# Joins of tiles 0 to 2 moved behind the branch, in front of the additions of their selected rows

## The chip, the cores and the metric

The kernel runs on one core of a Trainium2 chip. Its time is the device time in microseconds of one execution; the figure for a kernel is the median of its timed runs. TensorE does the matrix products, VectorE, ScalarE and GpSimd the elementwise work, and SP, a queue of its own, issues most of the DMA transfers. GpSimd issues the indirect ones. Each engine works through its own instructions in their written order, and waits at an instruction until the counters that it names (semaphores) have been reached.

## What is computed

Three stages follow each other on 2304 tokens of 512 values: attention, a mixture of eight experts, and a gated feed-forward layer. The change lies where the second stage passes into the third.

```
out = x.copy()
xc = x[x @ w_skip > 0]
e_idx, gate_w = ...                      # best expert of each token and its weight
for e in range(8):
    mask = e_idx == e
    h = np.maximum(xc[mask] @ w1[e], 0.0)
    y[mask] = gate_w[mask, None] * (h @ w2[e])
out[x @ w_skip > 0] = xc + y             # second stage
g = out @ w_gate
return (silu(g) * (out @ w_val)) @ w_out # third stage
```

## The kernel before

The tokens lie in 18 tiles of 128. Each expert has room for 192 of them. Its results are written to a table `ys` in HBM, one row for each place, and come back to the tokens' order by a gather.

**The last expert.** Its 192 rows are a short part (64 rows, product `yb`) and a long part (128 rows, product `ya`, made in two halves of 256 columns). Each product is copied to SBUF by `y_put_short` (on VectorE) or `y_put_long` (on ScalarE), and from there SP writes it to `ys`; the first write of `yb` and those of `ya` stand in SP's order behind the earlier gathers, which read the same table. So that tiles 0 to 2 need not wait for these writes, their rows of the last expert are not gathered: `sel_y` makes two fp16 parts of each product (`sely`; the high part on ScalarE, the rest on VectorE), and `sel_p(i)` picks the rows by a product with a matrix of zeros and ones (`selx`) on TensorE.

**A tile is put together in two steps.** The *join* `xp_1(i)` adds the gathered rows of the first seven experts, times the gate's weight, to the tokens; the addition at the end of `sel_p(i)` adds the selected rows of the last expert to the same tile `xr[i]`:

```
def xp_1(i):
    t = xg[i]
    dve.scalar_tensor_tensor(out=t if i > 2 else xr[i], in0=t, scalar=gw[:, i:i + 1], in1=xr[i], ...)   # L1213
def sel_p(i):
    p = bank([128, DM], "selx")          # eight products of 256 columns, L1132 and L1134
    ...
    dve.scalar_tensor_tensor(out=xr[i], in0=p, scalar=gw[:, i:i + 1], in1=xr[i], ...)                   # L1135
def y_put_long(e, o, n):
    t = t2.tile([128, n], F32, tag="t2", name="ya")
    hi_(t, yp.pop((e, 0)), 2.0 ** -8)    # copy on ScalarE, L340
    sp.dma_start(out=ys[r:r + 128, o:o + n], in_=t)                                                     # L1096
```

**Behind the branch.** A branch (L1599) asks whether an expert has more than 192 tokens; it is not taken here. Behind it tile 0 is transposed on TensorE (`xp_p`, product `xpp`), copied to `xpT` in fp16 by ScalarE (`xp_h`), and the rest of the rounding is put beside it by VectorE (`xp_l`); then come `gvp`, the projections of the third stage (`gv_part`, 128 tokens at a time for the first block), and so on for tiles 1 and 2. GpSimd gathers the rows of tiles 3 and up (`xp_g`).

**Conversion steps.** The third stage's weights are doubles and are turned into two fp16 parts on the way. A step `conv_next` works on three pieces at once: ScalarE rounds the piece finished by VectorE and GpSimd takes its rest (`w`), VectorE puts together the second (L1166 and L1167, `stg` and `cb`), ScalarE scales the third (L1159, L1160).

**What sets the order.** This part is written out by hand: each engine gets its instructions in the order of the code. Buffers come from pools. The pool `t2` has 24, for gathered rows, `sely`, `ya`, `yb` and others; a new tile takes a buffer that is free by then in the code's order, and its first writer waits for all who used that buffer before, for DMAs by the counter of their queue. SP's DMAs use the counters DMAHW0 to DMAHW7 in turn, GpSimd's DMASW0 to DMASW7.

Of the kernel before, what the change touches and what calls it, by code (L numbers as in the profile page):

```python
# [307 lines left out]
def body(ctx, tc, qkt, vwin, vrow, w_skip, w_gate, w1, w2, g_w, v_w, o_w, cst, out, dbg=None):  # L308
# [78 lines left out]
    if True:  # L387
# [647 lines left out]
        def x_load(e):  # L1035
            t = m2.tile([128, 8, CAP], F16, tag="xe", name="xe")
            d = sp.dma_start_transpose(out=t, in_=xs[e * CAP:(e + 1) * CAP, :])
            rows_ready(d)
            xe[e] = t

        def h_step(e, m):
            if m == 0:
                hT[e] = pools["h6"].tile([128, 2, 8, CAP], F16, tag="h6", name="hT")
            p = bank([128, CAP], "hp")
            n = 0
            for kk in range(4):
                for wl, xl in ((0, 0), (0, 4), (1, 0)):
                    pe.matmul(out=p, lhsT=wt[e, kk][:, wl, m * 128:(m + 1) * 128], rhs=xe[e][:, xl + kk, :],  # L1048
                              start=(n == 0), stop=(n == 11))
                    n += 1  # L1050
            hi_(hT[e][:, 0, m, :], p, 1.0, AF.Relu)
            lo_(hT[e][:, 1, m, :], p, hT[e][:, 0, m, :], 0.0, ALU.max)

        def h_first():
            hT[0] = pools["h6"].tile([128, 2, 8, CAP], F16, tag="h6", name="hT")
            p = [bank([128, CAP], "hp") for m in range(8)]
            for kk in range(4):
                for m in range(8):
                    for n, (wl, xl) in enumerate(((0, 0), (0, 4), (1, 0))):
                        pe.matmul(out=p[m], lhsT=wt[0, kk][:, wl, m * 128:(m + 1) * 128], rhs=xe[0][:, xl + kk, :],  # L1060
                                  start=(kk == 0 and n == 0), stop=(kk == 3 and n == 2))
                w_step()
            for m in range(8):
                hi_(hT[0][:, 0, m, :], p[m], 1.0, AF.Relu)
                lo_(hT[0][:, 1, m, :], p[m], hT[0][:, 0, m, :], 0.0, ALU.max)
                if m in (1, 5):
                    w_step()
# [33 lines left out]
        def sel_make():  # L1101
            f = slp.tile([128, 3], F32, name="idf")
            dve.tensor_copy(f, idx[:, 0:3])
            d = t2.tile([128, 4, 128], F16, tag="t2", name="seld")
            pool.memset(d[:, 3, :], 1.0)
            for i in range(3):
                dve.tensor_scalar(out=d[:, i, :], in0=ident, scalar1=f[:, i:i + 1], scalar2=None, op0=ALU.mult)
            sel["d"] = d
# [18 lines left out]
        def sel_p(i):  # L1127
            p = bank([128, DM], "selx")
            for c in range(2):
                o = slice(256 * c, 256 * c + 256)  # L1130
                for n in range(2):
                    pe.matmul(out=p[:, o], lhsT=sel["o"][:, 0, i, :], rhs=sel[0][:, n, o], start=(n == 0), stop=False)  # L1132
                for n in range(2):
                    pe.matmul(out=p[:, o], lhsT=sel["o"][:, 1 + c, i, :], rhs=sel[1][:, n, :], start=False, stop=(n == 1))  # L1134
            dve.scalar_tensor_tensor(out=xr[i], in0=p, scalar=gw[:, i:i + 1], in1=xr[i], op0=ALU.mult, op1=ALU.add)  # L1135
            xg[i] = xr[i]
# [19 lines left out]
        def conv_a(kind, f, n):  # L1156
            t = sg64[kind, f, n].rearrange("p (c w) -> p c w", w=2)
            lo_w, hi_w = t[:, :, 0], t[:, :, 1]
            act.activation(out=hi_w.bitcast(F32), in_=hi_w.bitcast(F32), func=AF.Copy, scale=2.0 ** -111)  # L1159
            act.activation(out=lo_w, in_=lo_w.bitcast(U32), func=AF.Copy, scale=LOW_S, bias=LOW_B)  # L1160
            return cbp.tile([128, 512], I32, tag="cb", name="cb")

        def conv_b(kind, f, n, b):
            t = sg64.pop((kind, f, n)).rearrange("p (c w) -> p c w", w=2)
            lo_w, hi_w = t[:, :, 0], t[:, :, 1]
            dve.scalar_tensor_tensor(out=lo_w, in0=hi_w, scalar=-0x80000000, in1=lo_w, op0=ALU.bitwise_and, op1=ALU.bitwise_or)  # L1166
            dve.scalar_tensor_tensor(out=b, in0=hi_w, scalar=3, in1=lo_w, op0=ALU.logical_shift_left, op1=ALU.bitwise_or)  # L1167

        def conv_c(kind, f, n, b):
            if n == 0:  # L1170
                wm[kind, f] = (wq if nw[0] % 18 < NPRE else wps[0]).tile([128, 2, 2, 512], F16, tag="w", name="w")
                nw[0] += 1
            w, bf = wm[kind, f], b.bitcast(F32)
            hi_(w[:, 0, n, :], bf, 1.0)
            rest_(pool, w[:, 1, n, :], bf, w[:, 0, n, :])
# [7 lines left out]
        def loads64(q=sp):  # L1183
            while lq and nld[0] - ncv[0] + len(sg64) < 6 and len(lq) > keep[0]:
                load64(*lq.pop(0), q=q)

        def conv_next(ld=True):
            c = st_b.pop() if st_b else None
            b = st_a.pop() if st_a else None
            if c:  # L1190
                conv_c(*c)
            if b:
                conv_b(*b)
                st_b.append(b)
            if cq:
                a = cq.pop(0)
                st_a.append(a + (conv_a(*a),))
            if ld:
                loads64()
# [11 lines left out]
        def xp_1(i):  # L1211
            t = xg[i]
            dve.scalar_tensor_tensor(out=t if i > 2 else xr[i], in0=t, scalar=gw[:, i:i + 1], in1=xr[i], op0=ALU.mult, op1=ALU.add)  # L1213
            blk, o = divmod(i, 3)
            if o == 0 and i:
                xpT[blk] = pools["h6"].tile([128, 8, BLK], F16, tag="h6", name="xpT")

        def xp_p(i):
            p = bank([128, 4, 128], "xpp")
            for kk in range(4):  # L1220
                pe.transpose(out=p[:, kk, :], in_=xg[i][:, 128 * kk:128 * kk + 128], identity=ident)  # L1221
            xs_[i] = p
# [319 lines left out]
        def w_step():  # L1542
            if ncv[0] < 8 * E:
                w_conv(*divmod(ncv[0], 8))
                ncv[0] += 1
                loads()

        loads()
        for e in range(E):
            last = e == E - 1  # L1550
            if not last:
                x_load(e + 1)
            if e == E - 3:
                sel_make()
            if e == 0:
                h_first()
            for m in range(8 if e else 0):
                h_step(e, m)
                if m % 2:
                    w_step()  # L1560
                if last and m in (1, 4):
                    conv_next()
                if last and m == 1:
                    for i in range(3):
                        xp_g(i)
            if e == E - 3:
                sel_turn()
            y_short(e)
            if last:
                most = nc.values_load(flagi[0:1, 0:1], min_val=0, max_val=NT)  # L1570
                conv_next()
                sel_y(1, 0)
                y_put_short(e)
                for i in range(3):
                    xp_1(i)
                y_long(e, 0, DM // 2)
                sel_y(0, 0)
                y_put_long(e, 0, DM // 2)
                y_long(e, DM // 2, DM // 2)
                sel_y(0, DM // 2)  # L1580
                y_put_long(e, DM // 2, DM // 2)
            else:
                for n in range(3 if 0 < e < E - 3 else 2):
                    w_step()
                y_put_short(e)
                if e == E - 2:
                    conv_next(False)
                y_long(e, 0, DM)
                w_step()
                w_step()  # L1590
                y_put_long(e, 0, DM)
                if e == E - 2:
                    keep[0] = 0
                    conv_next()
# [11 lines left out]
        for i in range(3, 6):  # L1606
            xp_g(i)
        pp = [bank([128, BLK], "gvp") for n in range(2)]
        conv_next(False)
        sel_p(0)  # L1610
        sel_p(1)
        xp_p(0)
        xp_h(0)
        xp_l(0)
        sel_p(2)
        for i in range(3):
            if i < 2:
                xp_p(i + 1)
                xp_h(i + 1)
            gv_part(0, 0, pp, 128 * i, 128)  # L1620
            if i < 2:
                xp_l(i + 1)
# [49 lines left out]
        for n, (kind, b, f) in enumerate(seq):  # L1672
# [33 lines left out]
            if n in (4, 6, 8):  # L1706
                i = 4 + n // 2
# [53 lines left out]
```

## Time and profile before

| | us |
|---|---|
| Median of 3 runs | 748.16 (747.73 to 748.56) |
| Profiled execution | 746.42 |
| Its span, first to last instruction | 744.6 |
| TensorE busy | 704.0 |
| VectorE busy | 498.7 |
| ScalarE busy | 386.7 |

Positions in the trace are counted from the start of the span. The branch is passed at about 325 us. An engine's busy time is that of its instructions; waiting is not in it. The times of products on TensorE are modelled at their ends, so that an engine that looks busy may be held up a little more or less than shown.

### The profile page before, as it was taken

What the parts mean: (1) busy time and instruction counts of PE and PEld (TensorE: products, weight loads), DVE (VectorE), ACT (ScalarE), POOL (GpSimd) and SP (SyncE); (2) the same over time, 40 slices, a digit from 0 to 9 for tenths busy, and PEclk for the clock granted to TensorE, in tenths of its full rate; (3) what the DMA queues carried; (4) which work ended last, traced back from release to release, by engine and by line L of the source; (5) the groups of instructions that cost most, each with busy time, mean ns of one, the idle gap of its engine ahead of it and who ended that gap; (6) DMA issues with size and microseconds to landing.
All of it is one profiled execution on the core that took longest, in us unless ns stands there. A gap on an engine that the chain in (4) does not pass through costs nothing.

```text
span 744.6 us, 16389 instructions
## 1 busy us (share of the span) xinstructions
PE 704.0 (95%) x6567; PEld 466.7 (63%) x6567; DVE 498.7 (67%) x940; ACT 386.7 (52%) x766; POOL 282.6 (38%) x261
## 2 busy tenths in 40 slices
PE   8889788889899999989999899999999999999997
PEld 6677677778777888766665554455666666544443
DVE  6677587777688788769888989976668886300000
ACT  6565475452577776647777752445555655300000
POOL 5345575354100000236886775234434454200000
PEclk9999899999999999999999999999999999999999
DMA  8889887571799999865766511840000000001001
GB/s 258 246 267 273 190 208 197 149 176 50 230 353 341 346 364 284 269 218 183 217 179 187 155 27 42 163 92 1 2 0 1 1 1 1 1 28 43 29 29 42
DMA packets 95334, 108.82 MB, mean 146 GB/s; under 512 B 51248, under 2 KB 68658, under 8 KB 94679
## 3 DMA queue, kind: packets, MB, share of 16 engines
q1 hardware_dynamic: 91319, 99.80, 46.5%
q0 software_dynamic: 2880, 6.89, 2.9%
q10 hardware_dynamic: 1056, 1.05, 0.5%
q8 instruction: 52, 0.85, 0.5%
q14 instruction: 27, 0.22, 0.1%
HBM read 81.69 MB, written 17.30 MB: 133 GB/s over the span
## 4 chain that ended last, share of the span: by engine, by line
PE 42%; DVE 9%; ACT 3%; issue 3%; POOL 0%; ACTq 0%; DVEq 0%; POOLq 0%
PE p L1430 19%; PE op L1513 19%; PE gvp L1257 3%; DVE cb L1167 2%; DVE stg L1166 2%; DVE sg L1270 1%; DVE yg L1213 1%; DVE xphl L346 1%; ACT u L340 1%; ACT stg L1159 1%; ACT sg L1265 0%; DVE xpT L346 0%; ACT stg L1160 0%; PE xpp L1221 0%; ACT xpT L340 0%
## 5 line engine op out<-in xcount | busy, mean ns | idle before, releaser
L1513 PE MATMUL op<-w,u 128*128 128x512 f16 x648 | 140.2, 379 | 0.0
L1257 PE MATMUL gvp<-xpT,w 128*128 128x384 f16 (+1 forms) x720 | 111.1, 315 | 4.5 <-ACT sg L1265 2.2
L1513 PEld LDWEIGHTS <-u 128*128 128x128 f16 x648 | 63.5, 98 | 76.2
L1257 PEld LDWEIGHTS <-w 128*128 128x128 f16 x720 | 67.6, 98 | 47.2 <-issue 5.5
L343 DVE SCALAR_TENSOR_TENSOR w<-stg,w 128x1024 f16<-128x1024 f32 x64 | 79.7, 1273 | 17.9 <-ACT w L340 17.8
L346 POOL TENSOR_TENSOR w<-cb,w 128x512 f16<-128x512 f32 x36 | 52.2, 1450 | 83.6 <-ACT w L340 83.6
L1430 PEld LDWEIGHTS <-w 128*128 128x128 f16 x528 | 51.6, 98 | 36.1 <-issue 2.1
L340 ACT ACTIVATE w<-stg 128x1024 f16<-128x1024 f32 x64 | 65.7, 1051 | 16.0 <-DMA stg<-in_moe_w 14.6
L1048 PEld LDWEIGHTS <-w 128*128 128x128 f16 x672 | 55.7, 98 | 1.7
L1048 PE MATMUL hp<-xe,w 128*128 128x192 f16 x672 | 56.6, 246 | 0.0
L340 ACT ACTIVATE y<-op 128x512 f32<-128x512 f32 x18 | 10.7, 592 | 84.9 <-PE op L1513 84.4
L1430 PE MATMUL p<-t,w 128*128 128x384 f16 x244 | 50.1, 326 | 1.6 <-DVE sc L1303 1.6
L1430 PE MATMUL p<-xpT,w 128*128 128x384 f16 x264 | 46.5, 326 | 0.0
L1167 DVE SCALAR_TENSOR_TENSOR cb<-stg 128x512 int32<-128x512 int32 x36 | 42.1, 1171 | 3.5
L1430 PE MATMUL p<-t,s7h 128*128 128x384 f16 x176 | 42.9, 326 | 1.1 <-ACT sa L1454 1.1
L1083 PE MATMUL ya<-w,hT 128*128 128x512 f16 (+1 forms) x216 | 42.9, 356 | 0.0
L346 POOL TENSOR_TENSOR u<-sa,u 128x384 f16<-128x384 f32 x22 | 20.1, 915 | 49.9 <-ACT u L340 49.9
L1430 PEld LDWEIGHTS <-s7h 128*128 128x128 f16 x264 | 25.8, 98 | 18.3 <-issue 1.3
L511 PE MATMUL qkd<-qks,identh 128*128 128x192 f16 x192 | 34.7, 350 | 2.0 <-issue 2.0
L539 POOL TENSOR_TENSOR vr<-vr 72x1024 f32<-72x1024 f32 x8 | 18.8, 2356 | 41.7 <-DMA vr<-in_vr 38.4
L411 PE MATMUL wbank<-wz 128*128 128x252 bf16 x209 | 30.9, 287 | 2.5 <-POOL wz L407 1.3
L1083 PEld LDWEIGHTS <-hT 128*128 128x128 f16 x216 | 20.5, 98 | 20.3 <-issue 1.6
(196 smaller groups left out, 1389.8 us busy)
## 6 DMA issues: line engine op xcount, KB each, us to landing
stg<-in_moe_w SPq DMA_DIRECT2D x64, 512.0 KB
qk<-in_qk SPq DMA_DIRECT2D x24, 384.0 KB
stg<-in_moe_w_out SPq DMA_DIRECT2D x12, 512.0 KB
stg<-in_moe_w_gate SPq DMA_DIRECT2D x11, 512.0 KB
stg<-in_moe_w_val SPq DMA_DIRECT2D x11, 512.0 KB
vw<-in_vw SPq DMA_DIRECT2D x18, 284.4 KB
vr<-in_vr SPq DMA_DIRECT2D x8, 576.0 KB
up<-outd SPq DMA_DIRECT2D x18, 256.0 KB
```

Of the source, the lines that this page charges most:

```text
L340: act.activation(out=o, in_=i, func=func, scale=s)
L343: dve.scalar_tensor_tensor(out=o, in0=i, scalar=s, in1=h, op0=op, op1=ALU.subtract)
L346: eng.tensor_tensor(out=o, in0=i, in1=h, op=ALU.subtract)
L411: pe.matmul(out=wbank[:, 260:512], lhsT=wz[:, 0:128], rhs=wz[:, 0:252], start=True, stop=True)
L511: pe.matmul(out=p[:, n], lhsT=identh, rhs=qk_at(u, n, m // 4).rearrange("p b (g r) -> p b g r", r=4)[:, :, :, m % 4], start=(m == 0), stop ...
L539: pool.tensor_tensor(out=r[:, 0:2], in0=r[:, 0:2], in1=r[:, 2:4], op=ALU.add)
L1048: pe.matmul(out=p, lhsT=wt[e, kk][:, wl, m * 128:(m + 1) * 128], rhs=xe[e][:, xl + kk, :], start=(n == 0), stop=(n == 11))
L1083: pe.matmul(out=p, lhsT=hT[e][:, hl, m, 0:128], rhs=w[:, o:o + n], **f)
L1167: dve.scalar_tensor_tensor(out=b, in0=hi_w, scalar=3, in1=lo_w, op0=ALU.logical_shift_left, op1=ALU.bitwise_or)
L1257: pe.matmul(out=pp[n][:, o:o + width], lhsT=w[:, wl, n, kk * 128:(kk + 1) * 128], rhs=xpT[blk][:, xl + kk, o:o + width], start=(j == 0), s ...
L1430: pe.matmul(out=p, lhsT=l(wl)[:, 128 * kk:128 * kk + 128], rhs=rr(xl, kk), start=first and j == 0, stop=last and j == 5, skip_group_check= ...
L1513: pe.matmul(out=p, lhsT=u[:, ul, t * 128:(t + 1) * 128], rhs=w[:, wl, f % 2, :], start=(n == 0), stop=(n == 3 * NF - 1))
```

## The change

The three joins `xp_1(0)` to `xp_1(2)` leave their place ahead of the branch, between the short rows' copy and the products of the long rows. Behind the branch the first two stand directly in front of their `sel_p`, the third ahead of tile 0's transposes, which come before `sel_p(2)`. The conversion step that opened that group now ends it.

```diff
@@ -1571,8 +1571,6 @@
                 conv_next()
                 sel_y(1, 0)
                 y_put_short(e)
-                for i in range(3):
-                    xp_1(i)
                 y_long(e, 0, DM // 2)
                 sel_y(0, 0)
                 y_put_long(e, 0, DM // 2)
@@ -1606,13 +1604,16 @@
         for i in range(3, 6):
             xp_g(i)
         pp = [bank([128, BLK], "gvp") for n in range(2)]
-        conv_next(False)
+        xp_1(0)
         sel_p(0)
+        xp_1(1)
         sel_p(1)
+        xp_1(2)
         xp_p(0)
         xp_h(0)
         xp_l(0)
         sel_p(2)
+        conv_next(False)
```

No operation is added or left out. The lines behind the first hunk have numbers two lower in the changed kernel as far as the second hunk.

VectorE, directly behind the branch, by the built program; `x` is the tile that is put together, `yg` the gathered rows, a minus marks rows of before, a plus those of the changed kernel.

```order
-L1166 SCALAR_TENSOR_TENSOR stg<-stg 128x512
-L1167 SCALAR_TENSOR_TENSOR cb<-stg 128x512
-L1135 SCALAR_TENSOR_TENSOR x<-selx,gw,x 128x512 x2
+L1597 UNCONDITIONAL_BRANCH x2
+L1213 SCALAR_TENSOR_TENSOR x<-yg,gw,x 128x512
+L1135 SCALAR_TENSOR_TENSOR x<-selx,gw,x 128x512
+L1213 SCALAR_TENSOR_TENSOR x<-yg,gw,x 128x512
+L1135 SCALAR_TENSOR_TENSOR x<-selx,gw,x 128x512
+L1213 SCALAR_TENSOR_TENSOR x<-yg,gw,x 128x512
 L346 TENSOR_TENSOR xpT<-xpp,xpT 128x4x128
 L1135 SCALAR_TENSOR_TENSOR x<-selx,gw,x 128x512
+L1166 SCALAR_TENSOR_TENSOR stg<-stg 128x512
+L1167 SCALAR_TENSOR_TENSOR cb<-stg 128x512
 L346 TENSOR_TENSOR xpT<-xpp,xpT 128x4x128 x2
```

The first three joins now alternate with the additions, and the conversion's two rows (L1166, L1167) come after the third addition.

ScalarE, ahead of the branch, before: the high parts `sely` and the copies `ya` of the two halves of the long rows, with the counters that each waits for.

```order
L340 ACTIVATE sely<-yb 128x256 [waits DMAHW6_49,PE_49]
L340 ACTIVATE sely<-ya 128x256 [waits DMAHW6_49,PE_49,Activation_49]
L340 ACTIVATE ya<-ya 128x256 [waits DMASW2_49,DVE_49]
L340 ACTIVATE sely<-ya 128x256 [waits PE_49]
L340 ACTIVATE ya<-ya 128x256 [waits DMASW0_49,DMASW3_49,DVE_49,Pool_49]
```

ScalarE at the same place in the changed kernel:

```order
L340 ACTIVATE sely<-yb 128x256 [waits DMAHW6_49,PE_49]
L340 ACTIVATE sely<-ya 128x256 [waits DMAHW6_49,PE_49,Activation_49]
L340 ACTIVATE ya<-ya 128x256 [waits DMAHW5_49,DMAHW4_49,DMAHW7_49,DMAHW0_49,DVE_49]
L340 ACTIVATE sely<-ya 128x256 [waits PE_49]
L340 ACTIVATE ya<-ya 128x256 [waits DMAHW1_49,DVE_49]
```

The five instructions stand in the same order, but the two copies `ya` wait for other counters: the first for four of SP's DMA counters instead of one of GpSimd's, the second for DMAHW1.

SP at the same place in the changed kernel: a load of weights, the two writes of the short rows, and the two of the long rows. Each write also waits for the counter that it will itself raise, where that is not known to have been reached.

```order
L1145 DMA stg<-in_moe_w_val 128x4x256 [waits DMAHW0_49,DMAHW6_49,DVE_49,Activation_49]
L1090 DMA ys<-yb 64x256 [waits DMASW3_49,DMASW4_49,DMASW2_49,DVE_49]
L1090 DMA ys<-yb 64x256
L1096 DMA ys<-ya 128x256 [waits DMAHW1_49,Activation_49]
L1096 DMA ys<-ya 128x256 [waits DMAHW2_49,Activation_49]
```

These rows are the same before the change. The counters are taken in turn, so that the load raises DMAHW6, the writes of `yb` DMAHW7 and DMAHW0, and those of `ya` DMAHW1 and DMAHW2. The copy `yb` itself, on VectorE, waits for DMAHW5 and DMAHW4 in both kernels.

## Rows read from the trace of the kernel before

**Rows 1.** Page, part 1: each engine's busy time, share of the span, instructions.

```profile
PE 704.0 (95%) x6567; PEld 466.7 (63%) x6567; DVE 498.7 (67%) x940; ACT 386.7 (52%) x766; POOL 282.6 (38%) x261
```

**Rows 2.** Chain of waits behind the branch and later: start us, length us, what.

```profile
326.88 1.47 DVE x L1135 x2
...
328.37 0.04 ACTq L340
...
329.24 0.70 DVE xpT L346
...
423.67 15.76 PE gvp L1257 x96
```

**Rows 3.** Timeline, TensorE's later gaps: start, length, instruction, [idle before, releaser].

```profile
409.63 6.01 PE L1257 MATMUL gvp<-xpT,w 128*128 128x384 f16 x36 [0.95 <-ACT sg L1265]
416.38 6.01 PE L1257 MATMUL gvp<-xpT,w 128*128 128x384 f16 x36 [0.73 <-DVE sg L1270]
423.67 1.62 PE L1257 MATMUL gvp<-xpT,w 128*128 128x384 f16 x9 [1.29 <-ACT sg L1265]
```

**Rows 4.** Timeline, VectorE around the branch.

```profile
320.76 0.74 DVE L1213 SCALAR_TENSOR_TENSOR x<-yg,gw,x 128x512 f32<-128x512 f32 x1
...
322.85 0.75 DVE L1213 SCALAR_TENSOR_TENSOR x<-yg,gw,x 128x512 f32<-128x512 f32 x1 [0.23 <-DMA yg<-ys,idx]
323.52 0.42 DVE L343 SCALAR_TENSOR_TENSOR sely<-ya,sely 128x256 f16<-128x256 f32 x1
...
325.47 0.69 DVE L1166 SCALAR_TENSOR_TENSOR stg<-stg 128x512 int32<-128x512 int32 x1 [0.38 <-DVEq L1599]
...
333.93 0.69 DVE L346 TENSOR_TENSOR xpT<-xpp,xpT 128x512 f16<-128x512 f32 x1 [2.75 <-ACT xpT L340]
```

**Rows 5.** Timeline, ScalarE around the branch.

```profile
320.66 0.38 ACT L340 ACTIVATE sely<-ya 128x256 f16<-128x256 f32 x1 [2.02 <-issue]
323.97 0.39 ACT L340 ACTIVATE ya<-ya 128x256 f32<-128x256 f32 x1 [2.93 <-DVE sely L343]
...
325.17 0.38 ACT L340 ACTIVATE ya<-ya 128x256 f32<-128x256 f32 x1 [0.54 <-issue]
...
333.30 0.60 ACT L340 ACTIVATE xpT<-xpp 128x512 f16<-128x512 f32 x1 [3.02 <-PE xpp L1221]
```

**Rows 6.** SP's writes to `ys`, by tile (first and last start) and timeline.

```profile
L1090 SPq DMA_DIRECT2D ys<-yb x16: 461/582/935, 207.9 to 323.4; - x16
L1096 SPq DMA_DIRECT2D ys<-ya x9: 338/387/927, 210.7 to 325.6; - x9
...
324.38 1.54 SPq L1096 DMA_DIRECT2D ys<-ya  x2
```

**Rows 7.** Timeline, TensorE around the branch.

```profile
323.03 1.02 PE L1031 MATMUL warm<-cs 128*128 128x406 bf16 x5
325.65 0.38 PE L1132 MATMUL selx<-sely,sel 128*128 128x256 f16 x2 [1.60 <-ACTq L1599]
...
326.52 0.38 PE L1132 MATMUL selx<-sely,sel 128*128 128x256 f16 x2
```

**Rows 8.** Windows, all engines: last columns granted clock, DMA share, GB/s.

```profile
323.00:324.00 1.00, 1.00 (x7) 0.41 (x5) 0.94 (x2) 0.03 (x1) 0.00 (x0) 1.00 1.11 358
...
327.00:328.00 1.00, 0.87 (x9) 0.57 (x7) 1.00 (x2) 0.52 (x1) 0.00 (x0) 1.00 0.06 19
```

**Rows 9.** Timeline, GpSimd: the third gather's issue.

```profile
315.58 0.94 POOL L1205 DMA_INDIRECT yg<-ys,idx  x1 [0.30 <-issue]
```

**Rows 10.** DMA issues: times issued, median us from issue to landing.

```profile
xs<-xhl,idx POOLq DMA_INDIRECT x18, 2.6
```

**Rows 11.** Windows, TensorE alone: length, busy us, granted clock, DMA share, GB/s.

```profile
74.05:77.46 3.41, 1.76 (x38) 1.00 1.04 274
77.46:80.87 3.41, 3.41 (x49) 0.50 0.41 97
...
323.21:326.62 3.41, 1.81 (x14) 1.00 0.71 219
```

## The prediction

> **What bounds the kernel now.** I read the page first: TensorE is busy for 704.0 of the 744.6 us [rows 1]. Almost any stretch in which it waits is therefore lost to the end, and the question is what it waits for around the branch. The chain of waits answers that: just behind the branch it runs over two additions of selected rows on VectorE, ScalarE's waits, the first copy into `xpT` and its rest on VectorE; it stays mostly with VectorE and ScalarE until 423.67 us, and from there it is TensorE [rows 2]. So whatever delays the restart behind the branch delays the end, unless a later gap takes it up. Between 408 and 424 us TensorE waits three more times, 0.95, 0.73 and 1.29 us, for VectorE and ScalarE [rows 3], that is for the same chain.
>
> Then the timelines of the engines ahead of the branch. On VectorE the first of the three joins starts at 320.76, the last at 322.85, after 0.23 us of waiting for its gather; the rest of the first half of the long rows, `sely`, whose copy ScalarE ended at 321.04, starts only at 323.52 [rows 4, 5]. ScalarE's copy `ya` of that half starts at 323.97, that of the second half at 325.17, after which the branch comes [rows 5]. SP issues the second of the two writes of the short rows at 323.4, the two writes of the long rows at 324.38 and 325.6 [rows 6]. TensorE ends its warming products at 324.05 and starts the selection products at 325.65, released by ScalarE's end of the branch [rows 7].
>
> **What the joins cost ahead of the branch.** Taken alone, their removal lets VectorE's `sely` start at about 321.1. The second half's products end at about 323.2, where the warming products follow [rows 7]; copy, rest and copy then give the second `ya` at about 324.1 instead of 325.17, and the branch comes 1.1 us earlier.
>
> **What the change adds without saying so.** The first `ya` must wait for a buffer. The joins used to read gathered tiles of the pool `t2`, and the first `ya` took the buffer that the first join had just freed; its wait was the gather's counter and VectorE. With the joins later, no such buffer is free. The built program now lets it wait for DMAHW5, DMAHW4, DMAHW7, DMAHW0 and VectorE. The first two are the counters for which VectorE's `yb` waited, so it is the buffer of `yb`, and DMAHW7 and DMAHW0 are those of the two writes that read `yb`. The second `ya` waits for DMAHW1, the counter of the first `ya`'s write: the same buffer once more. What was three copies in a row becomes write, copy, write, copy, with each write landed before the next copy.
>
> First write: SP issues the second write of `yb` at 323.4 as before, since it waits for the gathers, not for the joins [rows 6]. How long it flies no row shows. From below: the last write of all, issued at 325.6, has landed by 328.37, when ScalarE's waits behind the branch begin to pass [rows 2, 6]: 2.8 us at most, with the DMA share falling to 0.06 [rows 8]. From above: the third gather, whose issue ended at 316.52, let its join start at 322.85 [rows 4, 9]: 6.3 us with the DMA engines full. The write of `yb` is issued with the share still at 1.11, and four us later it is 0.06 [rows 8], so it is nearer to the lower bound: I take 3.4 us, hence 326.8. The first `ya` starts 2.8 us later than now.
>
> Second write: the first `ya` takes 0.4 us to its write's issue (323.97 to 324.38) [rows 5, 6], at 327.2. Nothing else moves then (0.06) [rows 8]. From above 2.8 us, as worked out; from below 1.6, the scatters' 2.6 from issue to landing [rows 10] less the 1.0 that the issue itself takes on GpSimd [rows 9]. I take 2.3. The second `ya` starts at 326.8 + 0.4 + 2.3 = 329.5 instead of 325.17: **4.3 us later**, and the branch with it. With both lower bounds it is 328.2 and 3.0 us, with both upper ones 332.9 and 7.7 us. Queued behind the waiting copies on ScalarE are the copy into `sely` of the second half, the branch and all copies into `xpT`; TensorE's selection products wait for ScalarE's end of the branch, GpSimd's next gathers and SP's next loads for the last write.
>
> The Trainium skill (DMA: Bandwidth & Descriptors, section "Anatomy of one DMA — SWDGE (gpsimd) path") gives a fixed cost of about 2.0 us to each DMA, most of it the receipt of the write, plus bytes over 436 GB/s. By it, as an estimate, the writes fly 2.15 and 2.3 us, the second `ya` starts at 328.3 and is 3.1 us late, and the whole sum below would be 1.2 us smaller, about 752.3. It was measured for GpSimd's path; no run here shows the two flights apart.
>
> **The joins behind the branch.** In the trace the first addition starts 1.23 us after the first selection product and the rest of `xpT` 2.36 us after that, held by ScalarE's copy [rows 2, 7]. Now the first join is done under the wait, but addition, join, addition, join stand ahead of that rest: 4 x 0.74 = 3.0 us [rows 2, 4]. That is **0.6 us more**. It hides the landing of the last write, which frees ScalarE at about 329.9 + 2.8 + 0.2 = 332.9, against 334.2 for the rest.
>
> The conversion step moved to the end of the group costs nothing that I can find. On VectorE it is two operations of one shape, 0.69 us each [rows 4]; it goes into the 2.75 us that VectorE now idles before the third rest [rows 4]. On ScalarE its three operations go between the first and second copy into `xpT`, and the third copy comes after 3.02 us of idle time [rows 5]. Without that cover it would be 1.4 us. GpSimd's rest of the weight may overlap it and stretch it, which the cover also holds.
>
> **TensorE's clock.** TensorE would be idle from 324.05 to about 330. In the windows of this trace the granted clock was 0.50 from 77.46 on, after 3.41 us in which TensorE was busy 1.76 us, while after 1.81 us around the branch it stayed at 1.00 [rows 11]. I expect the lower of the two levels, 1.2 GHz, for at least a part of the selection products. Eight of them take 0.87 us now (325.65 to 326.52) [rows 7]; at half speed the first addition comes 0.9 later and the second 0.1 more. So 0 to 1.0 us, by where the stretch ends; I take **0.4 us**.
>
> **Sum.** 4.3 + 0.6 + 0.4 = 5.3 us. Against the profiled execution, 746.42 us with its 1.8 us around the span, that is 751.7. That execution lies 1.7 below the median of the three timed runs, 748.16, so 5.3 on the median is **753.5 us**, slower by 0.7%.
>
> **Rivals.**
> *As the source reads (not slower).* The buffer's wait is over before ScalarE comes to it. Then the branch comes 1.1 us earlier, the joins give back 0.5 or so, and the time is 747.6. For it speaks only the idle time on VectorE. It decides itself at a flight of 0.6 us for the second write of `yb` (323.4 to 323.97); no row has a DMA as short. Chance 0.03.
> *A gap takes it up.* The three gaps of 2.97 us together [rows 3] are TensorE's wait for VectorE. If VectorE caught up over the 80 us before them, TensorE's own delay would be all that is left, 5.3 - 3.0 = 2.3 us: 750.5. Against it: the chain runs over VectorE itself from the restart to 423.67 [rows 2], so VectorE is as late as TensorE. Chance 0.06.
> *The clock stays low.* If the projections on the first block (three times 24 products, 128 columns) also run at 1.2 GHz, or both writes fly as long as their upper bounds, it is 7.7 + 0.6 + 1.0 = 9.3 at the worst, and some 8 in the middle: 756.2. Against it: the products fill TensorE once they run. Chance 0.07.
> My forecast, two write flights in the chain, has the remaining 0.84.
>
> **Range.** The lower bounds give 3.0 + 0.6 = 3.6 us, 751.8; the upper ones 757.5, which both writes must reach together. I give 751.3 to 756.0, which leaves out the first two rivals and half of the third, 0.13, and what little of the forecast lies outside. This kernel's measurement can tell about 0.2%, 1.5 us, from no change. Faster by more than that: 0.02 (the first rival would need more than its 1.1 us). Within: 0.04, the rest of that rival and the low edge of the second. Slower: 0.94.
>
> **What the changed profile would show.** ScalarE's first `ya` at about 326.8 with some 5 us of idle time before it, ended by a DMA; the second at about 329.5, again after a DMA; SP's two writes of the long rows 2.7 us apart instead of 1.2. TensorE idle for about 6 us instead of 1.60 ahead of `selx`, and a granted clock of 0.5 there. VectorE's joins and additions alternating; the first rest of `xpT` about 5 us later. Joins that vanish without a wait on ScalarE, or writes that land in under 1.6 us, would prove me wrong, and so would gaps at 408 to 424 us that shrink by as much as the restart is late.

## The result, and the profile after

The changed kernel takes **753.54 us** (median of 19 runs) against 748.16 for the kernel before (19 runs): the ratio is 1.0065, with a 95% interval of 1.0048 to 1.0082, so it is slower by 4.9 us, 3.6 to 6.1. The ratio is taken without one run of the changed kernel, 759.65 us, which counts as a slow run, and it is not the quotient of the two medians, which differ by 5.4 us.

The two profiled executions at first say something else; that of the changed kernel, 747.40 us, is the fastest of its 19. The page of the changed kernel gives, below its span, each engine's busy time and share:

```profile
span 745.6 us, 16391 instructions
...
PE 704.6 (95%) x6567; PEld 467.9 (63%) x6567; DVE 497.3 (67%) x940; ACT 386.5 (52%) x766; POOL 282.6 (38%) x261
```

The span is only 1.0 us longer than before and TensorE is as busy as in [rows 1]. The reason stands ahead of the change, where both kernels run the same code. In the timeline of before, the last expert's first product `ya` on TensorE, the third transpose `xpp` and the first `sg` on ScalarE, the first step of the third stage behind its projections, stand here:

```profile
317.79 5.40 PE L1083 MATMUL ya<-w,hT 128*128 128x256 f16 x48
...
331.26 0.61 PE L1221 MATMUL xpp<-cs,x 128*128 128x128 f32 x4
...
341.58 0.49 ACT L1265 ACTIVATE sg<-gvp 128x384 f32<-128x384 f32 x1
```

TensorE's timeline of the changed kernel, around the branch:

```profile
314.62 5.40 PE L1083 MATMUL ya<-w,hT 128*128 128x256 f16 x48
319.85 1.02 PE L1031 MATMUL warm<-cs 128*128 128x406 bf16 x5
326.02 0.59 PE L1132 MATMUL selx<-sely,sel 128*128 128x256 f16 x2 [5.15 <-ACTq L1597]
...
327.68 0.63 PE L1132 MATMUL selx<-sely,sel 128*128 128x256 f16 x2
...
329.39 1.06 PE L1221 MATMUL xpp<-cs,x 128*128 128x128 f32 x4
...
333.59 0.61 PE L1221 MATMUL xpp<-cs,x 128*128 128x128 f32 x4
```

This execution came to `ya` 3.17 us earlier; two traces of one and the same kernel differ by more than that there (last section). So from here on places are counted from the start of the first product `ya`, and a kernel is judged by two distances: from there to the first `sg`, and from there to the end of the span. Before they are 23.79 and 426.8 us; after, 27.90 and 431.0. **The change costs 4.1 and 4.2 us** by this measure, inside the timed interval; 4.2 less 3.2 is the 1.0 by which the spans differ.

ScalarE's timeline of the changed kernel shows where they go:

```profile
323.33 0.38 ACT L340 ACTIVATE ya<-ya 128x256 f32<-128x256 f32 x1 [5.47 <-DMA ys<-yb]
323.61 0.38 ACT L340 ACTIVATE sely<-ya 128x256 f16<-128x256 f32 x1
325.54 0.38 ACT L340 ACTIVATE ya<-ya 128x256 f32<-128x256 f32 x1 [1.55 <-DMA ys<-ya]
330.61 0.60 ACT L340 ACTIVATE xpT<-xpp 128x512 f16<-128x512 f32 x1 [4.69 <-PE xpp L1221]
...
334.23 0.60 ACT L340 ACTIVATE xpT<-xpp 128x512 f16<-128x512 f32 x1 [0.90 <-PE xpp L1221]
...
342.52 0.49 ACT L1265 ACTIVATE sg<-gvp 128x384 f32<-128x384 f32 x1
```

The first `ya` is now released by the write of `yb`, where VectorE released it before [rows 5]; the second, which followed 1.20 us behind the first [rows 5], waits for the write of the first and follows 2.21 us behind. Counted from the first product, the first `ya` is 2.53 us late (8.71 against 6.18 us) and the second 3.54 (10.92 against 7.38).

SP's side is a row of the groups by tile (first and last start) and one of the timeline:

```profile
L1090 SPq DMA_DIRECT2D ys<-yb x16: 460/586/1399, 205.4 to 320.4; - x16
```

```profile
323.74 2.55 SPq L1096 DMA_DIRECT2D ys<-ya  x2
```

The second write of `yb` is issued at 320.4 and releases `ya` at 323.33: 2.9 us, of which SP's issue itself takes 1.4 (the 1399 ns in the row). The first write of `ya`, issued at 323.74, releases the next copy at 325.54: 1.8 us. Windows of all engines say what else flew (last columns: granted clock, DMA share, GB/s):

```profile
319.40:320.40 1.00, 1.00 (x10) 0.72 (x9) 0.00 (x0) 0.00 (x0) 0.00 (x0) 1.00 1.16 384
...
321.40:322.40 1.00, 0.00 (x0) 0.00 (x0) 0.00 (x0) 0.00 (x0) 0.00 (x0) 1.00 0.25 79
...
323.70:324.70 1.00, 0.00 (x0) 0.10 (x1) 0.42 (x1) 0.29 (x2) 0.00 (x0) 1.00 0.08 30
```

The write of `yb` is issued behind traffic that ebbs within two us; that of `ya` has the DMA engines nearly to itself.

VectorE's timeline, behind the branch:

```profile
324.92 0.75 DVE L1213 SCALAR_TENSOR_TENSOR x<-yg,gw,x 128x512 f32<-128x512 f32 x1 [0.47 <-DVEq L1597]
328.00 0.75 DVE L1135 SCALAR_TENSOR_TENSOR x<-selx,gw,x 128x512 f32<-128x512 f32 x1 [2.33 <-PE selx L1134]
328.67 0.74 DVE L1213 SCALAR_TENSOR_TENSOR x<-yg,gw,x 128x512 f32<-128x512 f32 x1
329.63 0.75 DVE L1135 SCALAR_TENSOR_TENSOR x<-selx,gw,x 128x512 f32<-128x512 f32 x1 [0.23 <-PE selx L1134]
330.30 0.74 DVE L1213 SCALAR_TENSOR_TENSOR x<-yg,gw,x 128x512 f32<-128x512 f32 x1
331.24 0.69 DVE L346 TENSOR_TENSOR xpT<-xpp,xpT 128x512 f16<-128x512 f32 x1 [0.20 <-ACT xpT L340]
```

The first join is done while TensorE still waits. From the first selection product (326.02) to the rest of `xpT` (331.24) it takes 5.22 us, where it took 3.59 before [rows 4, 7]: additions and joins alternate, and twice VectorE waits for TensorE's products, which run at half speed. The windows of TensorE show it (busy time, instructions, granted clock, DMA share, GB/s):

```profile
321.41:324.83 3.42, 0.00 (x0) 1.00 0.22 64
324.83:328.24 3.41, 2.22 (x11) 0.50 0.18 60
328.24:331.66 3.42, 3.42 (x18) 0.50 0.31 83
331.66:335.07 3.41, 2.59 (x36) 1.00 0.43 150
```

After the 5.15 us of idling the granted clock is 0.50, the 1.2 GHz level, for 6.83 us; eight selection products take 1.66 us (326.02 to 327.68) instead of 0.87 [rows 7].

TensorE's later gaps, which answer to [rows 3]:

```profile
410.58 6.01 PE L1257 MATMUL gvp<-xpT,w 128*128 128x384 f16 x36 [0.96 <-ACT sg L1265]
417.35 6.01 PE L1257 MATMUL gvp<-xpT,w 128*128 128x384 f16 x36 [0.76 <-DVE sg L1270]
424.65 1.62 PE L1257 MATMUL gvp<-xpT,w 128*128 128x384 f16 x9 [1.29 <-ACT sg L1265]
```

They are as long as they were, 3.01 us together against 2.97: none of the delay is taken up there.

### The profile page after: what moved, and what is told of

Same layout as the page of the kernel before. It is cut to its first block, busy times and chain, and to the rows that moved or that the text cites. A ratio compares the mean times of both kernels' runs of the same rounds, so it can differ in the third digit from the quotient of the medians.

```text
span 745.6 us, 16391 instructions
## 1 busy us (share of the span) xinstructions
PE 704.6 (95%) x6567; PEld 467.9 (63%) x6567; DVE 497.3 (67%) x940; ACT 386.5 (52%) x766; POOL 282.6 (38%) x261
## 4 chain that ended last, share of the span: by engine, by line
PE 42%; DVE 9%; ACT 3%; issue 3%; POOL 0%; ACTq 0%; DVEq 0%; POOLq 0%
PE p L1430 19%; PE op L1513 19%; PE gvp L1257 3%; DVE cb L1167 2%; DVE stg L1166 2%; DVE yg L1213 1%; DVE sg L1270 1%; DVE xphl L346 1%; ACT u L340 1%; ACT stg L1159 1%; ACT sg L1265 0%; DVE xpT L346 0%; ACT stg L1160 0%; PE selx L1132 0%; PE selx L1134 0%
## 5 line engine op out<-in xcount | busy, mean ns | idle before, releaser
L1167 DVE SCALAR_TENSOR_TENSOR cb<-stg 128x512 int32<-128x512 int32 x36 | 41.8, 1160 | 3.8 <-DVE stg L1166 0.5
```

## The experiments

The theory: the time is lost to the two waits on the buffer of `yb`, not to the joins' new place. The rivals: the joins behind the branch are themselves the cost, or TensorE's low clock is most of it, or the conversion step's place is. Distances are from the first product `ya`, in us, from one trace each; the ratio is against the kernel before, in the experiments on the same chip.

| kernel | first `ya` product at | second copy `ya` | first `sg` | end | time, ratio (95%) |
|---|---|---|---|---|---|
| before | 317.79 | 7.38 | 23.79 | 426.8 | 1 |
| changed | 314.62 | 10.92 | 27.90 | 431.0 | 1.0065 (1.0048 to 1.0082) |
| own_buffers | 320.43 | 6.31 | 21.90 | 425.0 | 0.9981 (0.9957 to 1.0005) |
| first_own | 320.61 | 8.52 | 24.71 | 427.8 | 1.0041 (1.0013 to 1.0069) |
| one_buffer | 324.28 | 11.35 | 27.20 | 430.2 | 1.0103 (1.0068 to 1.0138) |
| before_own | 320.83 | 7.41 | 23.79 | 426.8 | 0.9991 (0.9959 to 1.0023) |
| warm_25 | 322.61 | 10.67 | 26.87 | 429.9 | 1.0057 (1.0025 to 1.0089) |
| conv_only | 323.53 | 7.24 | 23.25 | 426.3 | 0.9988 (0.9958 to 1.0017) |
| joins_between | 321.72 | 6.31 | 22.72 | 425.8 | 0.9988 (0.9959 to 1.0017) |
| before_again | 324.66 | 7.35 | 23.61 | 426.6 | profile only |
| changed_again | 321.66 | 11.01 | 28.06 | 431.1 | 1.0060 (1.0036 to 1.0083) |
| own_buffers_again | 321.62 | 6.31 | 22.50 | 425.6 | 1.0001 (0.9980 to 1.0023) |

**The joins moved, without the waits.** In `y_put_long` of the changed kernel the last expert's tiles come from another pool:

```diff
-            t = t2.tile([128, n], F32, tag="t2", name="ya")
+            t = (pools["h6"].tile([128, n], F32, tag="h6", name="ya") if e == E - 1 else
+                 t2.tile([128, n], F32, tag="t2", name="ya"))
```

> The changed kernel, but the last expert's two copies ya get buffers of another pool, in which buffers are free, so that neither waits for a write. Joins and conversion step stay behind the branch. Read in the trace: the stretch from the first product ya of the last expert on TensorE to the first sg on ScalarE (L1265 in the changed kernel), 23.8 us in the kernel before and 27.9 in the changed one. If the cost lies in the waits for the writes: the stretch falls to 22.7 to 23.8 us, ScalarE's two ya stand 2.6 us apart with no DMA ending their wait, and the time is that of the kernel before or up to 1 us less (ratio 0.998 to 1.001). If the cost lies in the joins that VectorE now does behind the branch: the stretch stays at 27 to 28 us and the ratio at 1.005 to 1.007.

Timelines of this kernel, ScalarE, TensorE:

```profile
324.17 0.38 ACT L340 ACTIVATE ya<-ya 128x256 f32<-128x256 f32 x1 [0.49 <-DVE sely L343]
326.74 0.38 ACT L340 ACTIVATE ya<-ya 128x256 f32<-128x256 f32 x1 [0.49 <-DVE sely L343]
...
342.33 0.49 ACT L1266 ACTIVATE sg<-gvp 128x384 f32<-128x384 f32 x1
```

```profile
320.43 5.40 PE L1083 MATMUL ya<-w,hT 128*128 128x256 f16 x48
...
327.22 0.38 PE L1133 MATMUL selx<-sely,sel 128*128 128x256 f16 x2 [0.53 <-ACTq L1598]
```

With the same order of the joins, but no wait for a DMA, the whole loss is gone: 21.90 instead of 27.90 us to the first `sg`. And the branch comes 1.07 us earlier than before, as the removal of the joins alone should give. So the joins' place costs nothing net. In this trace it even gains 1.9 us, more than expected: 0.6 us of it are there at the first rest of `xpT`, and 1.4 come from the third copy into `xpT`, which the kernel before starts late (next section); a second trace, below, gains less.

**One wait of the two.** The same edit for the first half only (`e == E - 1 and o == 0`).

> The changed kernel, but only the first copy ya has a buffer of its own; the second takes the buffer of yb and waits for the two writes of yb alone. If each wait costs as worked out: the second ya starts 8.5 to 9 us after the first product ya (10.9 in the changed kernel, 6.3 with both in buffers of their own), and the stretch to the first sg is 24 to 25 us, ratio to the kernel before 1.000 to 1.003. If the second write's flight does not matter: as in the changed kernel, 27 to 28 us.

ScalarE's timeline:

```profile
324.35 0.38 ACT L340 ACTIVATE ya<-ya 128x256 f32<-128x256 f32 x1 [0.49 <-DVE sely L343]
329.13 0.38 ACT L340 ACTIVATE ya<-ya 128x256 f32<-128x256 f32 x1 [2.71 <-DMA ys<-yb]
```

Now the second half takes the buffer of `yb`. The wait moved there and is shorter, since `yb`'s writes fly while the second half is computed: 0.9 us lost up to the first `sg` in the trace, as expected, 3.1 us (1.0 to 5.2) in the timed runs, a ratio just above the 1.000 to 1.003 that was expected.

**The waits, without moving the joins.** In the kernel before, `y_put_short` keeps its tile `yb`, and the last expert's `ya` is written into it:

```diff
             t = t2.tile([128, DM // 2], F32, tag="t2", name="yb")
+            one[e] = t
...
-            t = t2.tile([128, n], F32, tag="t2", name="ya")
+            t = one[e] if e == E - 1 else t2.tile([128, n], F32, tag="t2", name="ya")
```

> The kernel before, joins ahead of the branch, but the last expert's yb and both ya are written into one buffer, which brings back the same two waits on the counters of SP's writes. If the waits for the writes are the cost: the stretch from the first product ya to the first sg grows from 23.8 to 26.5 to 28 us, ratio 1.004 to 1.006. If the joins behind the branch are: no change, 23.8 us, ratio 1.000.

ScalarE's timeline (`ya` now bears the name of `yb`'s tile):

```profile
333.42 0.38 ACT L340 ACTIVATE yb<-ya 128x256 f32<-128x256 f32 x1 [5.89 <-DMA ys<-yb]
335.63 0.39 ACT L340 ACTIVATE yb<-ya 128x256 f32<-128x256 f32 x1 [1.55 <-DVE stg L1167]
```

The joins stand ahead of the branch as before, and the loss is there: 3.4 us up to the first `sg`. The second wait is put down to VectorE in this row, but that operation runs behind the branch; the interval of 2.21 us is that of the changed kernel. The timed loss, 7.7 us (5.1 to 10.3), is larger than the trace's 3.4, and than the ratio of 1.004 to 1.006 that was expected; no row explains this, and only six executions of it are compared.

**Buffers alone.** The kernel before with the first experiment's edit.

> The kernel before, joins ahead of the branch, with the two copies ya in buffers of their own. If the joins ahead of sely hold the branch there, as read: no change, 23.3 to 24 us and ratio 0.999 to 1.001, so that what the variant with both changes gains (21.9 us) comes from moving the joins. If the buffers themselves gain: below 23 us.

23.79 us to the first `sg`, as before, and no change in time that can be measured. Own buffers are worth something only where the joins are moved.

**TensorE kept busy in the wait.** In the changed kernel the warming products are issued five times over (their output is not used):

```diff
-        warm(WG)
+        for n in range(5):
+            warm(WG)
```

> The changed kernel with 25 warming products ahead of the branch instead of 5, so that TensorE is busy some 4 us longer while it waits. If the lower clock behind the idle time is a term of the sum: the granted clock stays at 1.00 around the branch, the additions of the selected rows come 0.7 to 1.0 us earlier, the stretch falls from 27.9 to 27.0 to 27.5 us, ratio to the kernel before 1.004 to 1.006. If the clock costs nothing at the end: the stretch stays at 27.9 us. If the clock is the main cost and the waits are hidden: it falls below 25 us.

TensorE's timeline, one of its windows, and the first rest of `xpT` on VectorE:

```profile
327.85 4.46 PE L1031 MATMUL warm<-cs 128*128 128x406 bf16 x25
333.76 0.38 PE L1132 MATMUL selx<-sely,sel 128*128 128x256 f16 x2 [1.46 <-ACTq L1598]
```

```profile
332.60:336.00 3.40, 2.20 (x19) 1.00 0.17 56
```

```profile
337.74 0.69 DVE L346 TENSOR_TENSOR xpT<-xpp,xpT 128x512 f16<-128x512 f32 x1
```

The wait is still there (second copy at 10.67 us), and the clock stays at 1.00. The way from the first selection product to the rest of `xpT` falls from 5.22 to 3.98 us, so the low clock costs 1.24 us there and the joins the other 0.39 over before's 3.59. Other traces agree: the second one of the changed kernel has 5.22 too, and own_buffers, first_own and own_buffers_again, with the joins at the same place and these products at full speed, 3.98 to 4.05. Of the 1.24 some 0.8 are left at the first `sg` (26.87 instead of 27.90, a little below the 27.0 to 27.5 expected; of the difference 0.25 come from an earlier second copy). The timed ratio can't tell this kernel from the changed one.

**The conversion step alone.** The kernel before with `conv_next(False)` behind `sel_p(2)`.

> The kernel before with the conversion step alone put last in its group, joins ahead of the branch. If the step is hidden in either place: 23.3 to 24 us for the stretch, ratio 0.999 to 1.001. If its two operations on VectorE delay the rests of xpT: 24.5 to 25.5 us.

0.4 to 0.5 us less to the first `sg` than in the two traces of before, a little less than expected, and nothing that can be measured in the time. Neither place of the step costs anything that shows.

**Joins behind the writes.** The kernel before with `xp_1(0)` and `xp_1(1)` behind the first `y_put_long`, `xp_1(2)` behind the second, the buffers of the first experiment, the conversion step last.

> A version to beat both: joins ahead of the branch, but two of them behind VectorE's rest of the first half of the long rows, and the third behind that of the second half; the copies ya in buffers of their own as in the first run; the conversion step last in its group. If VectorE's joins ahead of sely are what holds the branch before: the branch comes 1.0 us earlier than in the kernel before, the stretch is 22.0 to 23.2 us, ratio 0.997 to 0.9995. If something else holds the restart (the last write's landing, a transpose): 23.5 us or more, ratio 1.000.

22.72 us to the first `sg`, between the kernel before and own_buffers, and the second copy 1.07 us earlier than before, both as expected; the time can't be told from before's.

**The three that matter, once more.** The kernel before by a profile alone, the changed kernel and own_buffers timed on one chip, unchanged.

> The kernel before once more, for a second trace. In its first trace ScalarE's copy of tile 2 into xpT started 1.44 us after the modelled end of its transpose on TensorE, in the trace of the changed kernel and of four variants 0.04 us after it. If that delay belongs to the order of the kernel before: 1 to 1.5 us again, and the stretch from the first product ya of the last expert to the first sg is 23.5 to 24 us. If it was a matter of that one execution: about 0.04 us and 22.3 to 22.7 us; then the changed kernel loses 5.2 to 5.5 us in this stretch, not 4.1.

> The changed kernel once more, beside the version with its own buffers on one chip. In its first trace the granted clock was 0.50 from 10.2 to 17.0 us after the first product ya, and the stretch to the first sg was 27.9 us. If the lower clock's place shifts from execution to execution: the first addition of selected rows 1.1 to 2.0 us behind the first selection product, the stretch 27.0 to 28.0 us. If the waits had another size there: the second ya anywhere but 10.5 to 11.2 us after the first product ya. Ratio to the kernel before 1.004 to 1.008.

> The version with buffers of its own for both copies ya, once more. If its gain of 1.8 us in the first trace is its own: the stretch is 21.7 to 22.1 us again, and the ratio to the kernel before 0.996 to 0.999. If that was one execution's: 22.5 us or more, and a ratio of 0.999 to 1.001.

ScalarE in the second trace of the changed kernel:

```profile
330.46 0.38 ACT L340 ACTIVATE ya<-ya 128x256 f32<-128x256 f32 x1 [5.56 <-DMA ys<-yb]
332.67 0.38 ACT L340 ACTIVATE ya<-ya 128x256 f32<-128x256 f32 x1 [1.55 <-DMA ys<-ya]
```

The distances to the first `sg` repeat within 0.2 us for the kernel before (23.61 after 23.79) and the changed one (28.06 after 27.90), within 0.6 for own_buffers (22.50 after 21.90). So of the gain of own_buffers over the kernel before 1.1 to 1.3 us are left in the second trace and nothing in the time, which is the second of the two cases expected. The second copy `ya` at 11.01 us says that the waits had the same size again. On one chip the changed kernel is 0.60% slower and own_buffers is not: the loss comes with the waits and goes with them. None of the kernels is measurably faster than the one before.

## Why the prediction was right

**The mechanism held.** It forecast 753.5 us, in 751.3 to 756.0, by two flights of writes in the chain; own_buffers and one_buffer together show that these waits are the loss, and that the move of the joins without them is none. The rival "as the source reads" would have needed `ya` not to wait; it waited 5.47 us. "A gap takes it up" would have needed shorter gaps at 410 to 425 us; they are 3.01 us together, after 2.97. "The clock stays low" would have needed slow projections on the first block, or both writes near their upper bounds; the clock was back at 1.00 from 331.66 us, and the first `gvp` starts at 332.25.

**Where the sum stands, term by term**, counted from the first product `ya`:

- *First write.* 3.4 us were taken between 2.8 and 6.3; measured 2.9, near the lower bound, though it is issued while the DMA share is still near 1; 2.7 to 3.3 in the four other traces in which a copy waits for it. The first `ya` is 2.5 us late instead of 2.8.
- *Second write.* 2.3 us taken between 1.6 and 2.8; measured 1.8, and 1.8 again in changed_again, warm_25 and one_buffer. The two waits are 3.5 us together instead of 4.3: both terms were sized too far above their lower bounds, whose sum was 3.0. The Trainium skill (DMA: Bandwidth & Descriptors, section "Anatomy of one DMA — SWDGE (gpsimd) path") gave a fixed cost and a rate, from which 2.15 and 2.3 us were estimated for the two. The measured 2.9 and 1.8 lie on either side: the smaller write, of 64 KB, took longer than that of 128 KB, the opposite of what a fixed cost plus bytes gives, which was taken from GpSimd's path, where these writes are SP's. The DMA share, 1.16 ahead of the first and 0.08 around the second, may be why; no run takes size and company apart.
- *Joins behind the branch.* 0.6 taken, 0.4 measured with the clock at 1.00.
- *Clock.* 0.4 taken, with 1.0 as the upper bound; 1.24 measured up to the rest of `xpT`. The term was mis-sized where the bound was drawn from eight selection products: the clock stayed at 0.50 until 331.66 us, so the first transposes ran slowly too (four in 1.06 us instead of 0.66), and VectorE and ScalarE waited for them.
- *Conversion step.* 0 taken, and conv_only shows none.

At the rest of `xpT` that is 3.54 + 0.39 + 1.24 = 5.17 us (16.62 against 11.45), for a sum of 5.3: what the waits (0.8) and the joins (0.2) were given too much, the clock (0.8) was given too little. That the sum is right at this place is luck.

**What "carries over" missed.** The prediction took the delay at the restart to reach the end unreduced. It does not: 5.2 us at the first rest are 4.1 at the third copy into `xpT` (19.61 against 15.51), at the first `sg` and at the end. The gaps at 410 to 425 us have no part in it. In the kernel before that third copy starts 1.43 us after the modelled end of the transpose that it waits for (331.26 + 0.61 against 333.30 [rows 5]); in the changed kernel it starts 0.03 us after (333.59 + 0.61 against 334.23). So 1.4 us that the kernel before loses at this copy are not lost after the change: the delay is 5.5 us at the transpose (18.97 against 13.47) and 4.1 at the copy. The two second traces repeat it, with 5.79 and 4.45. The same lateness is in before_again, before_own and conv_only (1.2 to 1.5 us), and is 0.0 to 0.6 in all others. The order behind the branch alone does not make it: one_buffer has that of the kernel before and shows 0.04. What holds the copy there wasn't tried and stays open; ends on TensorE are modelled, so it may be the transpose or something else. The timed loss, 3.6 to 6.1 us, holds 4.1 as well as 5.3 and can't decide it. So the mechanism and the size of the loss were foreseen, but that the median came out at 753.54, next to the 753.5 of the forecast, is luck: the sum was 5.3 us, where the traces show 4.1 to 4.5 and the timed runs 4.9.

## What to carry to other kernels

When a step is moved later, ask who took the buffers that it used to set free: in a pool, the next tile may get one that a DMA still reads, and two copies in a row become write, copy, write, copy. The built order shows it before any run, as counters of other DMAs on the same instruction (here those of SP's writes in place of those of GpSimd's gathers); the cost is what of each write's flight nothing covers (flights of 2.9 and 1.8 us put the second copy 3.5 us back here), plus what TensorE's idling does to its clock. A buffer of its own for the copy removes it, but whether the move then pays must be measured: here it did not show in the time.

## What the runs showed of the hardware

- *Code that is the same reaches a point up to 10 us earlier or later.* All kernels do the same ahead of the first product `ya`. It starts between 314.62 and 324.66 us in the twelve traces, and at 317.79 and 324.66 in two of the same kernel. Eighty equal windows from 40 to 312 us show stretches at a granted clock of 0.50 in the lightly loaded part, as in [rows 11], but not the same ones each time. Window length times what the granted clock lacks of 1.00 adds up to 3.4 us in the first trace of the changed kernel, 5.1 and 10.3 in the two of before, 13.6 in that of conv_only. It is not all: the second trace of the changed kernel has 5.1 too and starts `ya` at 321.66. A difference of 4 us in this kernel is therefore read from a stretch, or from many timed runs, not from two spans.
- *TensorE came back at half speed.* After 5.15 and 5.24 us of idling both traces of the changed kernel show a clock of 0.50 around the selection products; after 0.5 to 2.8 us, in the other kernels, they ran at full speed (0.38 us a row). In one_buffer, after 5.57 us, the clock was low for only a part of them.
